# Pooled attention and a tanh-shrink layer on one core: the last two groups' sums on VectorE, the last group's output stored in parts

## The chip, the core and the metric

The kernel runs on one core of a Trainium2 chip. Its time is the device time of one execution in microseconds; lower is better. Where the text gives one number for a kernel, it is the median of its runs, or it is said to be that of the one execution that the profiler recorded. Engines go by their profile names: PE is TensorE (matmuls; PEld its weight loads), DVE is VectorE, ACT is ScalarE, POOL is GpSimd, SP is SyncE, which issues most DMAs.

## The reference

Attention whose keys and values are averaged over 8 neighbours, then a layer with the activation h - tanh(h). Cut to what matters:

```python
# q, k, v: (8, 8, 576, 64) float32;  w_in: (512, 2048);  w_out: (2048, 512)
k_p = k.reshape(B, H, S // 8, 8, D).mean(axis=3)
v_p = v.reshape(B, H, S // 8, 8, D).mean(axis=3)
scores = (1 / sqrt(D)) * q @ k_p.transpose(0, 1, 3, 2)
attn = softmax(scores)
x = (attn @ v_p).transpose(0, 2, 1, 3).reshape(B * S, H * D)   # (4608, 512)
h = x @ w_in
g = h - tanh(h)
out = g @ w_out                                                # (4608, 512)
```

## The kernel before

**Groups.** The 4608 rows of `x` are handled as nine groups of 512 tokens. Groups 0 to 7 hold the first 512 of the 576 tokens of each batch; group 8 holds the last 64 tokens of all eight batches. For each group g, TensorE makes the hidden layer (`h_mms`, line 425), 16 blocks of 128 hidden units; ScalarE takes the tanh of two blocks at a time and VectorE subtracts it (`h_act`, lines 438 and 439), which leaves `gT`: 128 partitions x 16 hidden blocks x 512 tokens in bf16. Then comes the output product with `w2b`. The attention of the next batch is woven in between by a plan written out by hand. Groups 7 and 8 have no next batch (`nb` is None), so their loops hold little but the layer itself.

**Seven products.** Groups 6, 7 and 8 (`SEVEN`) replace the eight quarter products of `g @ w_out` by seven. `gT` is cut into hidden halves (LO, HI) and token halves (C1, C2), `w2b` into hidden halves and column halves (C1, C2). Four sums of quarters of `gT` are needed, made by `g_sum` (line 527): sum 3 (S3), sum 2 (S2, which uses S3), sum 1 (S1), sum 4 (S4, which uses S2). The buffers S1 to S4 lie in `q_raw`. The seven products run on TensorE in the order 4, 2, 7, 1, 6, 5, 3 (`PRODUCTS`), each in two halves of 128 tokens, b = 0 and 1 (`product`, line 545: eight matmuls of 256 columns). Product 7 reads S3, product 6 reads S2, product 5 reads S1, product 3 reads S4. All but product 2 add up in one PSUM bank for each b; nothing is cleared after product 4, so that each bank holds a running sum. After every product the bank is read out (`evacuate`), and the next product on that bank adds to it only after that:

- products 4 and 7: ScalarE copies to `n0` and `n1` (line 560); product 2, which has its own bank, to `p2` (line 558);
- product 1: VectorE subtracts `n1` and writes columns C1 of `o_hs[0]` (line 572); `finish_11` then adds `p2` (line 578);
- product 6: ScalarE copies to columns C1 of `o_hs[1]` (line 562);
- product 5: VectorE subtracts `n0`, columns C2 of `o_hs[1]`; product 3: VectorE subtracts `n1`, columns C2 of `o_hs[0]` (both line 572).

`o_hs[0]` and `o_hs[1]` (shown as `o_h`) each hold one half of the group's output, 128 x 2 x 512 in float32, the middle index being b.

**The order around the change.** Each engine takes its instructions in the order of the program. Within a group of seven products, sum 3 is made while the last hidden blocks are finished. Sum 2 follows when the loop over products is at u = 2, and a manual dependency starts the two halves of sum 1 on GpSimd behind it. Sum 4 follows at u = 8, after both evacuations of product 1. `finish_11` runs on GpSimd, behind sum 1. In groups 6 and 7 each half of the output is stored by one DMA on SyncE's queue (`store_half`, line 588). Group 8's rows are scattered over the batches, and a store needs two DMAs, one for each 64 partitions (line 593): C1 of half 0 after `finish_11`, the whole of half 1 after product 5, both on SyncE, and C2 of half 0 after product 3, one DMA on SyncE and one on ScalarE's queue. That makes six DMAs, five of them on SyncE.

Of the kernel before, what the change touches and what calls it, by code (L numbers as in the profile page):

```python
# [15 lines left out]
B, H, S, D = 8, 8, 576, 64  # L16
POOL = 8
G = S // POOL
DM, DFF = 512, 2048
NHP = H // 2  # L20
R = 4
QA = 128 * R
# [4 lines left out]
NG = 9  # L27
# [4 lines left out]
NQ = NHID // 2  # L32
# [6 lines left out]
def kernel(  # L39
# [9 lines left out]
    nc = tc.nc  # L49
# [49 lines left out]
    o_hs = [const.tile([128, 2, DM], FP32, name=f"o_h{i}") for i in range(2)]  # L99
# [398 lines left out]
    C1, C2 = slice(0, HC), slice(HC, DM)  # L498
# [18 lines left out]
    def g_sum(n, i0, i1, eng=nc.vector):  # L517
        i = slice(i0, i1)
        a11, a12 = gT[:, NQ + i0 : NQ + i1, C1], gT[:, i, C1]
        a21, a22 = gT[:, NQ + i0 : NQ + i1, C2], gT[:, i, C2]  # L520
        o, x, y, op = {
            1: (S1, a21, a22, ALU.add),
            2: (S2, a22, S3[:, i, :], ALU.subtract),
            3: (S3, a11, a21, ALU.subtract),
            4: (S4, a12, S2[:, i, :], ALU.subtract),
        }[n]
        return eng.tensor_tensor(out=o[:, i, :], in0=x, in1=y, op=op)  # L527
# [46 lines left out]
    def finish_11(eng, plain=False):  # L574
        o = o_hs[0][:, :, C1]
        if plain:
            eng.tensor_tensor(out=o, in0=o, in1=n1, op=ALU.subtract)
        eng.tensor_tensor(out=o, in0=o, in1=p2, op=ALU.add)

    def finish_22(eng):  # L580
        o = o_hs[1][:, :, C2]
        eng.tensor_tensor(out=o, in0=o, in1=n0, op=ALU.subtract)

    def store_half(g, hf, cols=slice(0, DM), engs=(nc.sync, nc.sync)):
        o = o_hs[hf]
        if g < B:
            blk = out[g * S : g * S + QA, :].rearrange("(p j) m -> p j m", j=R)
            nc.sync.dma_start(out=blk[:, 2 * hf : 2 * hf + 2, cols], in_=o[:, :, cols])
            return
        tl = out.rearrange("(n t) m -> t n m", t=S)[QA:S, :, :]  # L590
        for e in range(2):
            n = 4 * hf + e
            engs[e].dma_start(
                out=tl[:, n : n + 3 : 2, cols], in_=o[64 * e : 64 * e + 64, :, cols]
            )

    def fill(n, bank, cols=512):
# [26 lines left out]
    for base, sign in ((G, 1), (-1, -1)):  # L624
        nc.gpsimd.affine_select(
            out=mask[:, :, :, 0],
            in_=mask[:, :, :, 0],
# [237 lines left out]
    for g in range(1, NG):  # L865
        nb = g + 1 if g + 1 < B else None
        more = nb is not None and nb + 1 < B

        tail = {2: 0, 3: 1, 5: 2, 7: 3}.get(nb)
        plan = {}  # L870
        if nb is not None:
            units = [(s_block(nb, j), av_block(nb), slot(4 * nb + j)) for j in range(4)]
            s_pairs, a_pairs = [0, 0, 0, 1, 2], [0, 1, 0, 2, 1]
            plan = {
                -12: [("s", 0)],
                -9: [("e", 0)],
                -8: [("s", 1)],
                -5: [("e", 1), ("t", 0)],
                -3: [("s", 2)],
                0: [("e", 2)],  # L880
                1: [("s", 3)],
                3: [("e", 3), ("t", 1)],
                4: [("a", 0)],
                5: [("a", 1), ("x", 0)],
                9: [("a", 2), ("a", 3), ("x", 1)],
            }
            if g == 1:
                plan[-10], plan[-7], plan[-5] = plan.pop(-12), plan.pop(-9), plan.pop(-8)
                plan[-2], plan[-1] = [("e", 1), ("t", 0)], plan.pop(-3)
            if tail is not None:  # L890
                units.append((s_tail(tail), av_tail(tail), slot_tl))
                plan[3].append(("s", 4))
                plan[4] += [("e", 4), ("t", 2)]
                if g == 1:
                    plan[6], plan[7] = plan[4][:1], plan.pop(5)
                    plan[4] = plan[4][1:]
                    plan[10] = plan.pop(9)
                plan[12] = [("a", 4), ("x", 2)]
            if g in SEVEN:
                plan = dict(PLAN7)  # L900
            xs = [x_pair(), x_pair(), x_tl]
        if nb is not None:
            pool_v(nb, nc.gpsimd)
        shs = {}

        def step(kind, n, bk=None):
            if kind == "t2":
                e_turn_dma(units[2][2], n, n + 1)
                return
            if kind == "t":  # L910
                e_turn_dma(units[2 * n][2], 0, 2 if n < 2 else 1)
                if tail and n == 0:
                    turn_tail(tail)
                return
            if kind == "x":
                x_turn_dma(xs[n], *((nb, 2 * n, 2) if n < 2 else (B, tail, 1)))
                return
            s, a, sl = units[n]
            if kind == "s" and bk:
                s_mms(s, bk)  # L920
                ng = s_max(bk)
                late.append(lambda: s_exp_heads(bk, ng, sl))
            elif kind in ("s", "sb"):
                bk = bk or PAIRS[s_pairs[n]]
                s_mms(s, bk)
                shs[n] = s_shift(bk)
            elif kind == "e":
                s_exp(shs[n], sl)
            else:
                bk = bk or PAIRS[a_pairs[n]]  # L930
                av_mms(sl, a, bk)
                normalise(bk, xs[n // 2][:, n % 2, :, :, :])

        for i in range(NHID):
            bk = HB[i // 2 % 3][i % 2] if g in SEVEN else i % 6
            h_mms(g, i, bk)
            if g in SEVEN and i == 15:
                for it in plan.pop(-1, ()):
                    step(*it)
            if i % 2:  # L940
                h_act(i - 1, bk - 1)
                if g in SEVEN:
                    if i in (3, 5) and carry:
                        carry.pop(0)()
                    for n, i0 in {13: [(3, 0)], 15: [(3, 4)]}.get(i, ()):
                        g_sum(n, i0, i0 + 4)
            for it in plan.get(i - NHID, ()):
                step(*it)
            if more and i in (13, 15):
                q_cast(nb + 1, se, i - 13, i - 11)  # L950
        for u in range(14 if g in SEVEN else 0):
            n, b = PRODUCTS[u // 2], u % 2
            product(n, b)
            evacuate(n, b, nb is not None)
            for it in plan.get(u, ()):
                step(*it)
                run_late()
            if u == 2:
                dep = g_sum(2, 0, NQ)
                after([g_sum(1, 0, 4, nc.gpsimd), g_sum(1, 4, NQ, nc.gpsimd)], dep)  # L960
            if u == 8:
                g_sum(4, 0, NQ)
            if b == 0:
                continue
            if n == "1":
                finish_11(nc.gpsimd, nb is not None)
                if g == NG - 1:
                    store_half(g, 0, C1)
            elif g == NG - 1 and n == "5":
                store_half(g, 1)  # L970
            elif g == NG - 1 and n == "3":
                store_half(g, 0, C2, (nc.sync, nc.scalar))
            elif n in "53":
                if n == "5" and nb is not None:
                    finish_22(nc.gpsimd)
                store_half(g, 0 if n == "3" else 1)
        if g in SEVEN and tail is not None:
            carry += [lambda i=tail: tail_values(i), lambda i=tail: x_turn_dma(x_tl, B, i, 1)]
        for u, (tb, qd) in enumerate(() if g in SEVEN else UNITS):
            o_mms(tb, qd * 4, qd * 4 + 4, 4 + tb % 2)  # L980
            if qd == 3:
                o_store(g, tb, 4 + tb % 2, se)
                run(stores)
            for it in plan.get(u, ()):
                step(*it)
            if u == 0 and more:
                pool_k(nb + 1, nc.gpsimd)
            if more:
                if u == 0:
                    q_turn_dma(nb + 1)  # L990
                    run(stores)
                if u == 4:
                    k_turn_dma(nb + 1)
                    k_place_kT(nb + 1, ge)
                if u == 11 and nb % 2 == 0:
                    run(tail_pieces(nb // 2))
                    tail_cast(nb // 2)
            if u == 13:
                load_for(g + 1)
            if g == SEVEN[0] - 1 and u >= 8 and w_ops:  # L1000
                w_ops.pop(0)()
# [29 lines left out]
```

## Time and profile before

| | us |
|---|---|
| median of three runs (lowest, highest) | 306.02 (305.19, 307.4) |
| the profiled execution, its own time | 306.24 |
| span of that execution, first to last instruction | 304.2 |
| TensorE matmul busy | 287.7 (95%) |
| VectorE busy | 202.8 (67%) |
| ScalarE busy | 145.0 (48%) |
| GpSimd busy | 135.4 (45%) |
| end of the last matmul | 297.9 |
| end of the last VectorE instruction | 298.4 |

Starts are counted from the first instruction. A line of the timeline gives start, duration, engine, source line, operation, what is written and what is read, the number of instructions that were merged into it, and in brackets the idle time of the engine before it and what ended that. The chain of waits follows the end of the run back from step to step to whatever released it. A line of a table of stretches gives the stretch, its length, the busy time of PE, PEld, DVE, ACT and POOL (with the number of instructions), the granted TensorE clock, the mean busy share of the 16 DMA engines and the rate in GB/s. For a source line with DMAs, the profile gives the time that the queue spent on issuing each, and the time from there to landing.

### The profile page before, as it was taken

How to read it: one execution, taken by the hardware profiler on the slowest of the kernel's cores; microseconds unless marked ns; L12 is line 12 of the kernel's file. 1: busy time of each engine (PE TensorE's matmuls, PEld its weight loads, DVE VectorE, ACT ScalarE, POOL GpSimd, SP SyncE). 2: the span in 40 equal slices, each digit the busy share in tenths (PEclk: the TensorE clock that was granted, in tenths of full speed). 3: DMA queues.
4: the chain of work that ended last, by engine and by line, in shares of the span. 5: the costliest groups of instructions: out<-in, count | busy, mean ns of one | idle time of the engine just before them, and what ended most of it. 6: DMA issues, size and time to landing. Idle time of an engine off the chain costs nothing.

```text
span 304.2 us, 4875 instructions
## 1 busy us (share of the span) xinstructions
PE 287.7 (95%) x1885; PEld 164.0 (54%) x1885; DVE 202.8 (67%) x283; ACT 145.0 (48%) x199; POOL 135.4 (45%) x112
## 2 busy tenths in 40 slices
PE   5779989899999999999999999999999999999991
PEld 1357865444454455445544454455447854874681
DVE  4586866549853993398329942986699847656861
ACT  2457755347523762366237623672366336416520
POOL 7544918308810692088107910791062920250080
PEclk9599999999999999999999999999999999999998
DMA  7999996789899999896799799959825540021005
GB/s 226 224 218 319 207 290 161 136 254 331 169 218 186 357 180 192 251 314 114 177 254 322 136 155 270 337 63 219 241 65 72 91 160 17 2 99 43 1 0 138
DMA packets 85383, 54.84 MB, mean 180 GB/s; under 512 B 60240, under 2 KB 73168, under 8 KB 85360
## 3 DMA queue, kind: packets, MB, share of 16 engines
q1 hardware_dynamic: 77696, 44.84, 58.7%
q0 software_dynamic: 6400, 8.91, 14.2%
q10 hardware_dynamic: 1264, 0.79, 0.9%
q8 instruction: 14, 0.23, 0.3%
q14 instruction: 9, 0.07, 0.1%
HBM read 36.70 MB, written 9.44 MB: 152 GB/s over the span
## 4 chain that ended last, share of the span: by engine, by line
PE 80%; DVE 10%; DMA 3%; ACT 3%; issue 1%; ACTq 0%; DVEq 0%
PE PS L425 31%; PE PS L468 26%; PE PS L545 11%; PE PS L378 4%; DVE gT L439 3%; PE PS L447 3%; PE PS L291 3%; DMA k_raw<-in_k_dram 2%; DVE sh L306 2%; DVE mx L303 2%; PE PS L272 2%; DMA xT<-x_sb 1%; PE PS L599 1%; DVE x_sb L400 1%; ACT E L342 1%
## 5 line engine op out<-in xcount | busy, mean ns | idle before, releaser
L439 DVE TENSOR_TENSOR gT<-PS,t_sb 128x1024 bf16<-128x1024 f32 x64 | 77.1, 1220 | 42.8 <-ACT t_sb L438 42.8
L425 PE MATMUL PS<-xT,w1b 128*128 128x512 bf16 x448 | 100.8, 379 | 1.0 <-DMA xT<-x_sb 0.9
L468 PE MATMUL PS<-w2b,gT 128*128 128x512 bf16 x384 | 89.8, 379 | 0.2 <-ACT v_sm L782 0.2
L438 ACT ACTIVATE t_sb<-PS 128x1024 f32<-128x1024 f32 x64 | 65.6, 1024 | 49.8 <-PE PS L425 48.4
L425 PEld LDWEIGHTS <-w1b 128*128 128x128 bf16 x512 | 49.1, 98 | 57.6 <-issue 1.9
L468 PEld LDWEIGHTS <-gT 128*128 128x128 bf16 x384 | 35.3, 98 | 37.7 <-issue 0.5
L224 POOL TENSOR_TENSOR v_raw<-v_raw 128x1280 f32<-128x1280 f32 x6 | 17.4, 2906 | 40.8 <-DMA v_raw<-in_v_dram 40.8
L489 ACT COPY o_h<-PS 128x512 f32<-128x512 f32 x22 | 12.8, 584 | 45.9 <-PE PS L468 45.8
L527 POOL TENSOR_TENSOR q_raw<-gT 128x1024 bf16<-128x1024 bf16 x6 | 12.6, 2122 | 44.3 <-PE PS L545 38.5
L303 DVE TENSOR_REDUCE mx<-PS 128x8 f32<-128x576 f32 x36 | 26.9, 748 | 5.8 <-PE PS L291 5.8
L342 ACT ACTIVATE E<-sh 128x576 bf16<-128x576 f32 x32 | 21.8, 680 | 18.5 <-DVE sh L306 18.5
L306 DVE TENSOR_TENSOR sh<-PS,mx 128x576 f32<-128x576 f32 x36 | 27.3, 757 | 1.2
L400 DVE TENSOR_TENSOR x_sb<-PS,rden 128x512 bf16<-128x512 f32 x32 | 22.1, 691 | 1.1
L399 DVE RECIPROCAL rden<-PS 128x8 f32<-128x8 f32 x36 | 7.3, 204 | 22.8 <-PE PS L378 22.7
L209 POOL TENSOR_TENSOR k_raw<-k_raw 128x1280 f32<-128x1280 f32 x7 | 20.3, 2904 | 0.1
L545 PEld LDWEIGHTS <-q_raw 128*128 128x128 bf16 x192 | 18.5, 98 | 2.6 <-DVE q_raw L527 0.4
L246 POOL COPY KB<-kT 64x288 bf16<-64x288 bf16 x12 | 5.1, 422 | 28.6 <-DMA kT<-kd 22.6
L260 ACT CAST q_bf<-q_raw 128x1024 bf16<-128x1024 f32 x14 | 14.4, 1038 | 5.6 <-DMA q_raw<-in_q_dram 5.6
L378 PEld LDWEIGHTS <-ET 128*128 128x128 bf16 x192 | 13.2, 98 | 5.3 <-ACT ET L361 0.8
L378 PE MATMUL PS<-VB,ET 128*128 128x130 bf16 (+2 forms) x192 | 15.8, 221 | 0.2 <-ACT ET L361 0.2
L447 PE MATMUL PS<-xT,w1b 128*128 128x256 bf16 x128 | 15.3, 273 | 0.7 <-ACT xT L417 0.7
L545 PEld LDWEIGHTS <-gT 128*128 128x128 bf16 x144 | 13.9, 98 | 2.0
(95 smaller groups left out, 294.4 us busy)
## 6 DMA issues: line engine op xcount, KB each, us to landing
k_raw<-in_k_dram SPq DMA_DIRECT2D x14, 512.0 KB, 8.5
out_dram<-o_h SPq DMA_DIRECT2D x26, 256.0 KB, 3.1
v_raw<-in_v_dram SPq DMA_DIRECT2D x12, 512.0 KB, 5.0
q_raw<-in_q_dram SPq DMA_DIRECT2D x11, 512.0 KB, 7.0
w1b<-in_moe_w_in_dram POOLq DMA_DIRECT2D x4, 512.0 KB, 8.9
q_raw<-in_q_dram POOLq DMA_DIRECT2D x2, 1024.0 KB, 14.8
w2b<-in_moe_w_out_dram POOLq DMA_DIRECT2D x4, 512.0 KB, 18.9
out_dram<-o_h SPq DMA_DIRECT2D x4, 512.0 KB, 2.8
```

The source lines that it names most:

```text
L209: eng.tensor_tensor(out=r[:, :, 0:4, :], in0=r[:, :, 0:4, :], in1=r[:, :, 4:8, :], op=ALU.add)
L303: nc.vector.reduce_max(out=mx.rearrange("p k h o -> p k (h o)"), in_=sc, axis=AX.X)
L306: nc.vector.tensor_tensor(out=sh[:, :, :, :], in0=sc, in1=mx.to_broadcast([128, 2, 4, G]), op=ALU.subtract)
L342: nc.scalar.activation(out=E[:, e, :, :].rearrange("p t c -> p (t c)")[:, 0:NK], in_=sh.rearrange("p k h c -> p (k h c)"), func=ACT.Exp, s ...
L378: nc.tensor.matmul(PS[ps, banks[half], D1 * h : D1 * (h + s1 - s0)], lhsT=ET[:, t, c0 : c0 + (ps.stop - ps.start)], rhs=VB[kb][:, t, s0:s1 ...
L400: nc.vector.tensor_tensor(out=x_sb, in0=ps[:, :, :, 0:D], in1=rden.to_broadcast([128, 2, 4, D]), op=ALU.mult,)
L425: nc.tensor.matmul(PS[:, bank, :].rearrange("p (j c) -> p j c", j=R), lhsT=w1b[:, fb, i * 128 : (i + 1) * 128], rhs=xT_of(g)[:, :, fb, :], ...
L438: nc.scalar.activation(out=t_sb[:, :, :], in_=ps, func=ACT.Tanh)
L439: nc.vector.tensor_sub(out=gT[:, i : i + 2, :], in0=ps, in1=t_sb[:, :, :])
L447: h_mm_last[0] = nc.tensor.matmul(PS[:, bank, 256 * s : 256 * s + 256].rearrange("p (j c) -> p j c", j=2), lhsT=w1b[:, fb, (2 * n + s) * 1 ...
L468: nc.tensor.matmul(PS[:, bank, 0 : c1 - c0], lhsT=gT[:, i, tb * 128 : (tb + 1) * 128], rhs=w2b[:, i, c0:c1], start=(i == 0), stop=(i == NH ...
L545: nc.tensor.matmul(ps, lhsT=A[:, i, 128 * b : 128 * b + 128], rhs=B_[:, i, :], start=(n in "24" and i == 0), stop=(i == NQ - 1), skip_grou ...
```

## The change

In the last two groups all of sums 2, 1 and 4 are made on VectorE, one after the other, directly behind the subtraction of the last two hidden blocks (i = 15) and sum 3; GpSimd makes no sum there. Group 6 keeps its order. In the last group, `finish_11` runs on VectorE, and the output is stored in parts: C1 of half 0 after product 1, C1 of half 1 after product 6, C2 of half 1 after product 5 (one DMA on SyncE, one on ScalarE), and C2 of half 0 for each b by itself after product 3's evacuation of that b (SyncE and ScalarE each). That makes ten DMAs, seven on SyncE and three on ScalarE. Groups 6 and 7 store as before.

```diff
--- before.py
+++ after.py
@@ -581,17 +581,18 @@
         o = o_hs[1][:, :, C2]
         eng.tensor_tensor(out=o, in0=o, in1=n0, op=ALU.subtract)
 
-    def store_half(g, hf, cols=slice(0, DM), engs=(nc.sync, nc.sync)):
-        o = o_hs[hf]
-        if g < B:
-            blk = out[g * S : g * S + QA, :].rearrange("(p j) m -> p j m", j=R)
-            nc.sync.dma_start(out=blk[:, 2 * hf : 2 * hf + 2, cols], in_=o[:, :, cols])
-            return
+    def store_half(g, hf):
+        blk = out[g * S : g * S + QA, :].rearrange("(p j) m -> p j m", j=R)
+        nc.sync.dma_start(out=blk[:, 2 * hf : 2 * hf + 2, :], in_=o_hs[hf][:, :, :])
+
+    def store_part(hf, cols, b0, b1, engs=(nc.sync, nc.sync)):
+
         tl = out.rearrange("(n t) m -> t n m", t=S)[QA:S, :, :]
         for e in range(2):
-            n = 4 * hf + e
+            n = 4 * hf + 2 * b0 + e
             engs[e].dma_start(
-                out=tl[:, n : n + 3 : 2, cols], in_=o[64 * e : 64 * e + 64, :, cols]
+                out=tl[:, n : n + 2 * (b1 - b0) - 1 : 2, cols],
+                in_=o_hs[hf][64 * e : 64 * e + 64, b0:b1, cols],
             )
 
     def fill(n, bank, cols=512):
@@ -944,6 +945,9 @@
                         carry.pop(0)()
                     for n, i0 in {13: [(3, 0)], 15: [(3, 4)]}.get(i, ()):
                         g_sum(n, i0, i0 + 4)
+                    if i == 15 and nb is None:
+                        for n in (2, 1, 4):
+                            g_sum(n, 0, NQ)
             for it in plan.get(i - NHID, ()):
                 step(*it)
             if more and i in (13, 15):
@@ -955,25 +959,28 @@
             for it in plan.get(u, ()):
                 step(*it)
                 run_late()
-            if u == 2:
+            if nb is not None and u == 2:
                 dep = g_sum(2, 0, NQ)
                 after([g_sum(1, 0, 4, nc.gpsimd), g_sum(1, 4, NQ, nc.gpsimd)], dep)
-            if u == 8:
+            if nb is not None and u == 8:
                 g_sum(4, 0, NQ)
-            if b == 0:
-                continue
-            if n == "1":
-                finish_11(nc.gpsimd, nb is not None)
-                if g == NG - 1:
-                    store_half(g, 0, C1)
-            elif g == NG - 1 and n == "5":
-                store_half(g, 1)
-            elif g == NG - 1 and n == "3":
-                store_half(g, 0, C2, (nc.sync, nc.scalar))
-            elif n in "53":
-                if n == "5" and nb is not None:
-                    finish_22(nc.gpsimd)
-                store_half(g, 0 if n == "3" else 1)
+            if g == NG - 1:
+                if n == "1" and b:
+                    finish_11(nc.vector)
+                    store_part(0, C1, 0, 2)
+                elif n == "6" and b:
+                    store_part(1, C1, 0, 2)
+                elif n == "5" and b:
+                    store_part(1, C2, 0, 2, (nc.sync, nc.scalar))
+                elif n == "3":
+                    store_part(0, C2, b, b + 1, (nc.sync, nc.scalar))
+            elif b:
+                if n == "1":
+                    finish_11(nc.gpsimd, nb is not None)
+                elif n in "53":
+                    if n == "5" and nb is not None:
+                        finish_22(nc.gpsimd)
+                    store_half(g, 0 if n == "3" else 1)
         if g in SEVEN and tail is not None:
             carry += [lambda i=tail: tail_values(i), lambda i=tail: x_turn_dma(x_tl, B, i, 1)]
         for u, (tb, qd) in enumerate(() if g in SEVEN else UNITS):
```

## The prediction

> **What bounds the kernel now.** Read first: the page's busy times, then the chain of waits from group 7 on.
>
> ```profile
> PE 287.7 (95%) x1885; PEld 164.0 (54%) x1885; DVE 202.8 (67%) x283; ACT 145.0 (48%) x199; POOL 135.4 (45%) x112
> ```
> ```profile
> 259.65 12.23 PE PS L545 x112
> 271.88 13.81 PE PS L425 x64
> 285.69 12.24 PE PS L545 x112
> 297.93 0.02 issue
> 297.96 0.42 DVE o_h L572
> ```
>
> TensorE is the bound: from 259.65 to 297.93 the chain holds nothing but matmuls. Any stall of TensorE in the products of group 7 or 8 therefore reaches the end in full. Behind the last matmul lie 0.45 us of VectorE and then 5.8 us (298.38 to 304.2) of stores and closing. Next, the timeline of group 8's products:
>
> ```profile
> 288.78 1.22 DVE L527 TENSOR_TENSOR q_raw<-gT,q_raw 128x2048 bf16<-128x2048 bf16 x1
> 290.17 4.20 POOL L527 TENSOR_TENSOR q_raw<-gT 128x1024 bf16<-128x1024 bf16 x2 [19.66 <-PE PS L545]
> 292.01 0.42 DVE L572 TENSOR_TENSOR o_h<-PS,k_raw 128x256 f32<-128x256 f32 x1 [2.01 <-PE PS L545]
> 292.51 3.66 PE L545 MATMUL PS<-k_raw,q_raw 128*128 128x256 bf16 x32
> 293.13 2.33 DVE L527 TENSOR_TENSOR q_raw<-gT,q_raw 128x2048 bf16<-128x2048 bf16 x1
> 294.32 2.26 POOL L578 TENSOR_TENSOR o_h<-o_h,k_raw 128x512 f32<-128x512 f32 x1
> 296.61 3.56 SPq L593 DMA_DIRECT2D out_dram<-o_h x5
> 297.96 0.42 DVE L572 TENSOR_TENSOR o_h<-PS,k_raw 128x256 f32<-128x256 f32 x1 [0.45 <-PE PS L545]
> 298.41 0.71 ACTq L593 DMA_DIRECT2D out_dram<-o_h x1
> ```
>
> In order: g_sum 2; g_sum 1 on POOL; the evacuation of product 1, b=0, for which VectorE had stood idle 2.01 us; products 6 and 5; g_sum 4; POOL's p2 addition; SP's five issues, which start only when that addition ends (294.32 + 2.26 = 296.58); the last evacuation; ScalarE's one issue. The stores by line, the first and the last one of SP, and DMA activity in quarter microseconds:
>
> ```profile
> L593 SPq DMA_DIRECT2D out_dram<-o_h x1: 685/685/685, 296.6 to 296.6; - x1
> DMA to landing us min/median/max: 2.5/2.5/2.5
> ```
> ```profile
> L593 SPq DMA_DIRECT2D out_dram<-o_h x1: 747/747/747, 299.4 to 299.4; - x1
> DMA to landing us min/median/max: 3.8/3.8/3.8
> ```
> ```profile
> 297.75:298.00 0.25, 0.17 (x2) 0.00 (x0) 0.04 (x1) 0.00 (x0) 0.00 (x0) 1.00 0.13 33
> 298.00:298.25 0.25, 0.00 (x0) 0.00 (x0) 0.25 (x1) 0.00 (x0) 0.00 (x0) 1.00 0.86 209
> 302.50:302.75 0.25, 0.00 (x0) 0.00 (x0) 0.00 (x0) 0.00 (x0) 0.00 (x0) 0.50 0.51 176
> 302.75:303.00 0.25, 0.00 (x0) 0.00 (x0) 0.00 (x0) 0.00 (x0) 0.00 (x0) 0.50 0.05 16
> ```
>
> The last two numbers of a row are DMA share and GB/s. A share of 0.13 in a quarter that then runs at 0.86 puts the first byte at 297.96; 0.05 in the last puts the end near 302.77. Between them all 1 MB of group 8's output moves, back to back. SP's last issue starts at 299.42 (296.61 + 3.56 - 0.75), 1.04 after its data was ready. It lands at 303.22; 0.98 of closing follows. So the tail is set by late stores, held up by POOL.
>
> **The sums (groups 7 and 8).** Both POOL sums go (4.20 a group); VectorE gets one sum of 128x2048, and g_sum 4 moves ahead of the evacuations. In the compiled order, both now stand before the evacuation of product 1, b=0. Price of each: 1.22, from g_sum 2, the same shape. Bounds: 1.22 is the shortest of the six such sums, and 2.33 the longest, which ran while POOL had its sums. I take 1.22, since POOL has no work then. VectorE starts back-to-back instructions 0.02 to 0.04 apart. Group 8: g_sum 2 ends at 290.00; + 2 x 1.22 + 0.09 = 292.53, against 292.01: the evacuation is 0.52 late. Behind it waits TensorE, since product 6, b=0, adds into that bank. Before, the evacuation ended at 292.43, and a hand-over from VectorE to TensorE takes 0.05 (group 6: g_sum 3 ends at 234.85, its weight load begins at 234.90), so 292.51 had 0.03 to spare: a stall of 0.49. Group 7 by the same rows: 262.74 + 1.23 = 263.97; + 2 x 1.23 + 0.09 = 266.52 against 265.97, less 0.03: 0.52. The b=1 evacuation adds nothing: 0.42 of VectorE against eight matmuls (0.87) on b=0. Together **+1.01 us on TensorE**; at 2.33 a sum it would be 2.71 + 2.74 = 5.45, at the other end (no stall) 0. POOL's relief is worth nothing on the path: S1 was ready in time (products 6 and 5 ran without a gap).
>
> **The p2 addition on VectorE (group 8).** Price 0.69:
>
> ```profile
> L209 DVE TENSOR_TENSOR k_raw<-k_raw x3: 426/686/692, 4.7 to 9.7; 128x512 f32<-128x512 f32 x2, 128x256 f32<-128x256 f32 x1
> ```
>
> With group 7's 0.52, product 1's evacuations run from 293.05 to 293.91, the addition to 294.64. VectorE's next work is product 5's b=0 at 295.38 + 1.01 = 296.39: that gap of 1.75 covers it; without cover it would cost 0.69. The first stores can be issued at 294.67 instead of 296.61.
>
> **The stores.** Six become ten, seven on SP and three on ScalarE, all in pieces of 1 KB. SP, at 0.60 to 0.75 an issue: C1 of half 0 from 294.67 to 295.95; C1 of half 1 (last evacuation at 294.46 + 0.37 + 1.01 = 295.84) to 297.3; C2 of half 1 (ready 296.63 + 1.01 = 297.64) from 297.67 to 298.3; C2 of half 0, b=0 (ready 298.51) from 298.54 to 299.2; b=1 (ready 298.38 + 1.01 = 299.39) from 299.42. ScalarE issues beside SP, at 0.71. By chance the last issue starts when it started before; what changes is how soon it lands. By the compiled order it also waits for the landing of C1's second store (295.3 + 2.5 = 297.8), past by then.
>
> Data starts 1.35 after issue (296.61 to 297.96), and 1 KB pieces move at some 195 GB/s (298 to 299.25, the C1 stores of before). C1: 296.02 to 297.36; half 1, C1: to 298.8; half 1, C2: 299.02 to 300.36; the last 256 KB: to 301.7, against 302.77. Landing 0.45 later (302.77 to 303.22): 302.15, which is 2.7 after issue instead of 3.8. From TensorE's end to the span's end it was 304.2 - 297.93 = 6.27; it becomes 0.45 of evacuation, 0.03 to the issue, 2.7 to the landing and 0.98 of closing, 4.16: **-2.1 us on the tail**. Bounds of the last landing: 2.5 (empty rings, first row) and 3.9 (ScalarE's store of before), so -2.3 to -0.9; I take 2.7, nearest to the first row, as the rings hold little when it is issued.
>
> Group 7's stores are issued 0.5 later with their evacuations; only group 8's evacuations into the same halves, 17 us on, wait for their landing (2.6 after issue): nothing.
>
> Here the Trainium skill (DMA: Bandwidth & Descriptors, Measured) speaks against the change: it advises batching to 1 MiB, and gives 0.95 us for 64 KB (there, of a load), the size of the last four stores. No run here shows a 64 KB store; four of 0.95 in turn would, as an estimate, end the data at 303.7 and the kernel near 307.2, while my rows give 305.1. Its mechanism is the fourth rival, priced there by rows.
>
> **Sum.** +1.01 - 2.1 = -1.1. The profiled execution took 306.24 (span 304.2, 2.04 around it); 306.24 - 1.1 = **305.1 us**, span 303.1. The median shown, 306.02, lies 0.2 below that execution; runs scatter from 305.19 to 307.4, so I leave it.
>
> **The rivals.**
> 1. No stall: VectorE would have to do each sum 0.26 faster than any row shows. Then -2.1: 304.1. Chance 0.10.
> 2. The last landing is no shorter, rings not drained: 3.8 again, 306.2. For it: ScalarE's store took 3.9 with 0.5 MB ahead; against it: half of the output is now away by 299. Chance 0.12.
> 3. Slower, from sums at 2.33 each: stalls of 5.45 less 2.1, so 309.5. It decides from stalls of 2.1 together, 1.5 a sum. For it: group 6's sum took 1.43 beside POOL; against it: POOL idle. Chance 0.06.
> 4. Slower, from small stores: the last four, of 64 KB, do not overlap, and each takes from first byte to landing as long as SP's first store (2.5 - 1.35 = 1.15). They begin at 299.9, so the last lands at 304.5: 304.5 + 0.98 + 2.04 = 307.5. It decides from 0.83 each, where the last lands at 303.22 as before. For it: GB/s falls with the piece (some 400 in group 7's 4 KB pieces, 195 at 1 KB); against it: the pieces of these stores stay at 1 KB, and the six stores of before moved back to back with no gap between them. Chance 0.10.
>
> The forecast keeps 0.62, its own range 304.3 to 305.9. The range reaches to rivals 1 and 2, with some scatter, and leaves out 3 and 4 (0.16): 303.8 to 306.9. About 1%, 3 us, is what a measurement of this kernel can tell from no change: faster by that needs rival 1 and a good run (0.03); slower is rival 3 and little else (0.07); within 0.90.
>
> **What would show it.** In the changed profile: two more 1.22 us rows at line 527 behind g_sum 2; the first line-572 row after them 0.5 late in both groups, and a gap of TensorE of 0.5 before product 6, released by VectorE; SP's first store at 294.7; the last landing about 2.7 after issue. No gap of TensorE, sums near 2.3, or a last landing over 3.5 would make the prediction wrong.

## The result and the profile after

The changed kernel takes 304.18 us (median of nine runs, 303.56 to 305.47); the kernel before took 305.57 us in nine runs (305.19 to 307.4). The ratio is 0.9949, 95% interval 0.9926 to 0.9971: 1.6 us faster by the ratio, between 0.9 and 2.3 (the medians alone differ by 1.4). That is a change of half a per cent, clear of the scatter of nine runs a side. The forecast was 305.1 with a range of 303.8 to 306.9, and no change to be told at 1%.

The profiled execution took 304.10 us, span 302.4 instead of 304.2. The page's busy times and the chain of waits, as shown of before:

```profile
PE 287.3 (95%) x1885; PEld 163.5 (54%) x1885; DVE 203.5 (67%) x286; ACT 144.9 (48%) x199; POOL 123.8 (41%) x107
```
```profile
259.34 12.37 PE PS L545 x112
271.71 13.81 PE PS L425 x64
285.52 12.38 PE PS L545 x112
297.91 0.02 issue
297.93 0.42 DVE o_h L572
```

POOL is busy 11.6 us less. The products of groups 7 and 8 take 12.37 and 12.38 instead of 12.23 and 12.24: TensorE does stall, by 0.14 in each group. After the last matmul 4.5 us are left instead of 6.3. The timeline of group 8's products (start, duration, what runs, idle time before and what ended it):

```profile
288.61 1.22 DVE L527 TENSOR_TENSOR q_raw<-gT,q_raw 128x2048 bf16<-128x2048 bf16 x1
289.75 1.22 DVE L527 TENSOR_TENSOR q_raw<-gT 128x2048 bf16<-128x2048 bf16 x1
290.89 1.22 DVE L527 TENSOR_TENSOR q_raw<-gT,q_raw 128x2048 bf16<-128x2048 bf16 x1
292.02 0.42 DVE L572 TENSOR_TENSOR o_h<-PS,k_raw 128x256 f32<-128x256 f32 x1
292.49 3.65 PE L545 MATMUL PS<-k_raw,q_raw 128*128 128x256 bf16 x32
293.07 0.69 DVE L578 TENSOR_TENSOR o_h<-o_h,k_raw 128x512 f32<-128x512 f32 x1
293.80 5.88 SPq L593 DMA_DIRECT2D out_dram<-o_h  x7
295.31 0.42 DVE L572 TENSOR_TENSOR o_h<-PS,k_raw 128x256 f32<-128x256 f32 x1 [1.54 <-PE PS L545]
296.64 2.76 ACTq L593 DMA_DIRECT2D out_dram<-o_h  x3
297.93 0.42 DVE L572 TENSOR_TENSOR o_h<-PS,k_raw 128x256 f32<-128x256 f32 x1 [0.45 <-PE PS L545]
```

Sums 2, 1 and 4 each last 1.22, but start 1.14 apart. The p2 addition ends at 293.76, and SP's first store goes out at once. SP's last store, and the DMA activity around it:

```profile
L593 SPq DMA_DIRECT2D out_dram<-o_h x1: 818/818/818, 298.9 to 298.9; - x1
DMA to landing us min/median/max: 2.3/2.3/2.3
```
```profile
298.75:299.00 0.25, 0.00 (x0) 0.00 (x0) 0.00 (x0) 0.00 (x0) 0.00 (x0) 1.00 0.98 332
299.00:299.25 0.25, 0.00 (x0) 0.00 (x0) 0.00 (x0) 0.00 (x0) 0.00 (x0) 1.00 0.14 41
299.25:299.50 0.25, 0.00 (x0) 0.00 (x0) 0.00 (x0) 0.00 (x0) 0.00 (x0) 1.00 0.21 66
300.50:300.75 0.25, 0.00 (x0) 0.00 (x0) 0.00 (x0) 0.00 (x0) 0.00 (x0) 1.00 0.64 160
```

Data now ends near 300.8 instead of 302.8. But the last evacuation ended at 298.35 and its store started only at 298.9, and from 299.0 to 299.5, before its data moved, the DMA engines ran nearly dry (0.14 and 0.21 busy). The pair before, for b=0, had taken SP 1.26 us and ScalarE 1.24 us to issue, where 0.6 to 0.75 had been expected.

Where the 1.8 us of span went, both kernels measured alike: group 7's first product starts 0.31 earlier (259.18 against 259.49), in a part that the change does not touch, so scatter; the two stalls cost 0.28; from the last matmul to the span's end it is 4.5 instead of 6.3, 1.8 less. The thirteen profiled executions of this document reach group 7 anywhere between 258.8 and 259.9, so the experiments are read by three lengths of their profiles: the two groups' products, the stretch from group 7's first product to the span's end (44.71 before, 43.22 after), and the tail from the last product's end. Spans are given to 0.1 us, so stretches and tails are good to 0.05.

### The profile page after: what moved, and what is told of

Its sections match the earlier page's. It is cut to its first block, busy times and chain, and to the rows that moved or that the text cites. A ratio compares the mean times of both kernels' runs of the same rounds, so it can differ in the third digit from the quotient of the medians.

```text
span 302.4 us, 4875 instructions
## 1 busy us (share of the span) xinstructions
PE 287.3 (95%) x1885; PEld 163.5 (54%) x1885; DVE 203.5 (67%) x286; ACT 144.9 (48%) x199; POOL 123.8 (41%) x107
## 3 DMA queue, kind: packets, MB, share of 16 engines
q1 hardware_dynamic: 77856, 44.71, 59.4%
## 4 chain that ended last, share of the span: by engine, by line
PE 79%; DVE 10%; DMA 5%; ACT 3%; issue 1%; ACTq 0%; DVEq 0%
PE PS L425 32%; PE PS L468 25%; PE PS L545 11%; PE PS L378 4%; PE PS L447 3%; DVE gT L439 3%; PE PS L291 3%; DMA k_raw<-in_k_dram 2%; DMA xT<-x_sb 2%; DVE sh L306 2%; DVE mx L303 2%; PE PS L272 1%; ACT E L342 1%; DVE x_sb L400 1%; ACT t_sb L438 1%
## 5 line engine op out<-in xcount | busy, mean ns | idle before, releaser
L291 PEld LDWEIGHTS <-qT 128*128 128x128 bf16 x128 | 9.9, 98 | 8.8 <-issue 1.6
```

## The experiments

Two theories were to be told apart. First: SP was held up by POOL, so that either edit that frees POOL or goes round it brings most of the gain. Second: the gain comes from storing in smaller parts. Later two more questions came up: why the stall was so small, and why one pair of stores was slow to issue. The edits are cut to the lines that change. All lengths stand in one table, in us; "load" says where a 16 KB packet of the instruction queue moved near the end, which is taken up below:

| kernel | stall, groups 7 / 8 | tail | stretch | median (ratio, interval) | load |
|---|---|---|---|---|---|
| before | 0 / 0 | 6.3 | 44.71 | 1 | after the span |
| changed | 0.14 / 0.14 | 4.5 | 43.22 | 304.18 (0.9949, 0.9926 to 0.9971) | in the stores |
| changed again | 0.14 / 0.14 | 4.25 | 42.96 | 304.05 (0.9936, 0.9924 to 0.9949) | in the stores |
| sums only | 0.14 / 0.14 | 5.0 | 43.71 | 305.19 (0.9973, 0.9958 to 0.9987) | not seen |
| stores only | 0 / 0.43 | 4.25 | 43.11 | 304.39 (0.9952, 0.9934 to 0.9969) | after the span |
| last block whole | 0.14 / 0.14 | 4.4 | 43.12 | 303.80 (0.9925, 0.9903 to 0.9948) | not seen |
| sum 4 late | 0 / 0 | 4.0 | 42.44 | 303.36 (0.9914, 0.9889 to 0.9940) | not seen |
| sum 4 late, again | 0 / 0 | 4.0 | 42.47 | 303.85 (0.9936, 0.9913 to 0.9960) | after the span |
| sum 4 late, last block whole | 0 / 0 | 4.4 | 42.82 | 303.91 (0.9923, 0.9902 to 0.9944) | after the span |
| sums in the order 2, 4, 1 | 0.27 / 0.26 | 4.0 | 42.97 | 304.60 (one run) | after the span |
| padded on GpSimd | 0.14 / 0.14 | 4.05 | 42.76 | 304.61 (one run) | after the span |
| padded on ScalarE | 0.14 / 0.14 | 4.0 | 42.69 | 304.26 (one run) | after the span |
| padded on TensorE | 0.14 / 0.14 | 4.8 | 43.51 | 304.76 (one run) | in the stores |

**The sums alone.** On the kernel before:

```diff
+                    if i == 15 and nb is None:
+                        for n in (2, 1, 4):
+                            g_sum(n, 0, NQ)
-            if u == 2:
+            if nb is not None and u == 2:
-            if u == 8:
+            if nb is not None and u == 8:
```

> The sums of groups 7 and 8 on VectorE as in the changed kernel, the stores and the p2 addition as before (POOL). Measure: the stretch from group 7's first product (line 545) to the span's end, 44.71 us before, 43.22 in the changed kernel. Theory 1 (what helps is that POOL, with no sums, releases SP earlier; parts of the output are of little account): stall of 0.14 a group, POOL's addition 1.27 from 293.1 on, SP's first store near 294.4, last pair at 298.4 with the rings half empty, stretch 43.4 to 43.6, ratio to before 0.9960. Theory 2 (the parts are what helps): the last store lands 3.8 after its issue as before, stretch 44.2 or more, ratio 0.999 to 1.001.

Timeline of this kernel:

```profile
293.63 1.27 POOL L578 TENSOR_TENSOR o_h<-o_h,k_raw 128x512 f32<-128x512 f32 x1 [24.86 <-DVE o_h L572]
294.92 4.57 SPq L593 DMA_DIRECT2D out_dram<-o_h  x5
```

POOL, without sums of its own to finish first, waits only for VectorE's evacuation, adds in 1.27 instead of 2.26, and SP starts 3.48 before the last matmul's end (298.40) where it was 1.31 before. The tail falls by 1.3 and the stretch by 1.0: 43.71 lies just above the first theory's 43.4 to 43.6 and well under the second's 44.2. The ratio, 0.9973, is weaker than its 0.9960, which the interval still holds.

**The stores and the addition alone.** On the changed kernel, the sums put back:

```diff
-                    if i == 15 and nb is None:
-                        for n in (2, 1, 4):
-                            g_sum(n, 0, NQ)
-            if nb is not None and u == 2:
+            if u == 2:
-            if nb is not None and u == 8:
+            if u == 8:
```

> The stores in parts and the p2 addition on VectorE as in the changed kernel, the sums as before (two on POOL, sum 4 after product 1). Theory 1: no stall of TensorE, the addition ends by about 294, SP is free as early as in the changed kernel: stretch 42.9, 0.3 below the changed kernel, ratio 0.9935. Theory 2 (VectorE and POOL in each other's way): the addition, with two operands in SBUF, waits for POOL's sums (to 294.4) and pushes sum 4 (before 295.46) towards product 3 (296.0): addition near 1.5 us, a gap of TensorE before product 3 of up to 0.8, stretch 43.3 to 43.8.

Timeline of this kernel, VectorE behind product 1 and TensorE at product 3:

```profile
292.95 1.67 DVE L578 TENSOR_TENSOR o_h<-o_h,k_raw 128x512 f32<-128x512 f32 x1
294.54 1.21 DVE L527 TENSOR_TENSOR q_raw<-gT,q_raw 128x2048 bf16<-128x2048 bf16 x1
295.68 0.74 DVE L572 TENSOR_TENSOR o_h<-PS,k_raw 128x256 f32<-128x256 f32 x2
296.14 1.91 PE L545 MATMUL PS<-w2b,q_raw 128*128 128x256 bf16 x16 [0.26 <-DVE o_h L572]
```

The addition takes 1.67 beside POOL's sums against 0.69 in the changed kernel, sum 4 and product 5's evacuation come late, and product 3 starts 0.43 late. So the second expectation names the mechanism, while the stretch, 43.11, falls between the two (42.9; 43.3 to 43.8). Still the tail falls by 2.0. The edits alone take 1.0 and 1.6 of stretch; both together take 1.5 (1.75 in the second profile, 2.0 in two padded kernels below). They do not add up, since both remove the same wait, SP's for POOL. But the parts count too: "sums only" has a tail of 5.0, the padded kernels, which have the same sums, 4.0. How much of that 1.0 belongs to the parts and how much to the addition on VectorE, no run here separates.

**The last block stored whole.** On the changed kernel:

```diff
-                elif n == "3":
-                    store_part(0, C2, b, b + 1, (nc.sync, nc.scalar))
+                elif n == "3" and b:
+                    store_part(0, C2, 0, 2, (nc.sync, nc.scalar))
```

> The changed kernel, but the last block (C2 of half 0) is stored as before, one pair of 128 KB after both evacuations of product 3. In the changed kernel the pair for b=0 took 1.25 us to issue on both queues, so that the last pair started at 298.9, 0.5 after its data. Theory 1 (the split by b gives nothing back): last pair at 298.4, landing 2.5 to 2.8 later, stretch 43.0 to 43.3. Theory 2 (the split helps): landing 3.3 or more after issue, stretch 43.7 or more.

Last pair at 297.98, landing 2.6 and 2.8 later, stretch 43.12: as the first theory has it, and beside this profile of the changed kernel the split gains nothing. The same edit without the stall, below, shows why that is not the whole answer.

**Sum 4 behind product 1's evacuation again.** On the changed kernel:

```diff
-                        for n in (2, 1, 4):
+                        for n in (2, 1):
-            if nb is not None and u == 8:
+            if u == 8:
```

> The changed kernel, but sum 4 stands behind the evacuations of product 1 again (on VectorE, alone). Theory: the gap of 0.14 before product 6 in each group comes from sum 4 ahead of the evacuation, so it goes: products of groups 7 and 8 12.24 each instead of 12.37, stretch 42.94, 0.28 below the changed kernel, tail unchanged at 4.5. Rival: product 1's evacuation is still late or sum 4 comes too late for product 3: stretch 43.2 or more.

The stall is gone in both groups, as expected: VectorE waits 0.87 for product 1 instead of being late. The tail was expected unchanged at 4.5 and came out at 4.0; here the pair for b=0 took 0.49 and 0.74 to issue. The changed kernel itself was therefore profiled once more.

**The changed kernel again, and the two variants beside it on one chip.**

> The changed kernel itself, for a second profile. In its first one the pair of stores for b=0 took 1.25 us to issue on both queues, and DMA activity sank to 0.14 of the engines at 299.0 before the last pair moved. Theory 1 (that belongs to the pattern: both queues issue small stores at the same instant): 1.2 us again, tail from TensorE's end 4.5. Theory 2 (a hiccup of that one execution, as the same pair took 0.49 and 0.74 with sum 4 late): 0.75 or less, last pair within 0.1 of its data, tail 4.0 to 4.2. Stall 0.14 a group either way.

The pair took 1.06 and 1.04, the last pair started 0.3 after its data, the tail was 4.25. So it recurs; the hiccup of one execution is out. The exact 1.2 and 4.5 do not recur.

> Sum 4 behind product 1's evacuation, and the last block stored whole, in one pair of 128 KB. Beside the kernel with sum 4 late alone, it prices the split by b without stall. Theory 1 (the split is worth what the smaller last pair lands earlier): last landing 2.7 after issue against 2.1, tail 4.3 to 4.4 against 4.0, median 0.3 to 0.5 above that kernel. Theory 2 (the split is worth nothing): tail 4.0 to 4.1, medians within 0.2.

(The edits of the two kernels above together.) Tail 4.4 against 4.0: the split by b is worth some 0.4 of stretch when the issue is not slow. The medians, 303.91 against 303.85, expected 0.3 to 0.5 apart, do not show it; its runs scatter from 303.0 to 305.4.

> The kernel with sum 4 late once more, beside the changed kernel on the same chip. Theory: no gap before product 6 (products 12.23 and 10.48), tail 4.0, median 0.3 us below the changed kernel if the slow issue was a hiccup, 0.8 below if it belongs to the changed kernel.

Products without a gap, tail 4.0, stretch 42.47 against 42.44 in its first profile. The median is 0.2 below that of the changed kernel beside it (303.85 and 304.05), below either figure expected, and the intervals overlap. By its profiles this version is 0.5 to 0.8 faster than the changed kernel; by medians the two are not told apart on that chip.

**The order of the sums.** On the changed kernel:

```diff
-                        for n in (2, 1, 4):
+                        for n in (2, 4, 1):
```

> The changed kernel with the sums in the order 2, 4, 1 in groups 7 and 8, so that sum 4, which reads sum 2's result, stands right behind it. Theory 1 (a VectorE instruction that needs nothing of the one before starts 0.09 before that one's end, one that does starts 0.04 after it): sum 2 to sum 4 1.26 instead of 1.14, evacuation 0.12 later, TensorE's gap 0.26 to 0.28 a group instead of 0.14. Theory 2 (instructions follow each other at 1.14 whatever they read): gap 0.14 as in the changed kernel.

Timeline of this kernel; the two sums of the first line are 2 and 4:

```profile
289.49 2.49 DVE L527 TENSOR_TENSOR q_raw<-gT,q_raw 128x2048 bf16<-128x2048 bf16 x2
291.89 1.22 DVE L527 TENSOR_TENSOR q_raw<-gT 128x2048 bf16<-128x2048 bf16 x1
293.02 0.90 DVE L572 TENSOR_TENSOR o_h<-PS,k_raw 128x256 f32<-128x256 f32 x2
```

Sum 4, which reads sum 2's result, no longer overlaps it (2.49 for the two); sum 1, which needs neither, starts 0.09 before their end (289.49 + 2.49 = 291.98). The stall grows to 0.27 and 0.26: the first theory, in its number.

**What makes the pair slow.** The DMA table of a stretch lists queues with packets, MB and share of the engines' time. In the changed kernel, from 297.00 to 297.25, and in its second profile, from 297.25 to 297.50, it has a line that the others lack there:

```profile
q8 instruction: 1, 0.02, 27.8%
```
```profile
q8 instruction: 1, 0.02, 21.9%
```

One packet of 16 KB of instructions, some 0.9 to 1.1 us on one DMA engine (27.8% of 16 engines for 0.25 us is 1.1; the table counts a packet whole in the stretch in which it starts). In the other kernels so far it moved after the span or not at all. Three kernels lengthen one engine's program behind all else, each by four idle instructions, to see whether the packet moves:

```diff
+    for _ in range(4):
+        nc.gpsimd.memset(zeros[0:1, 0:2], 0.0)
```

> The changed kernel with four tiny fills on GpSimd behind everything else, which only make its program longer. In both profiles of the changed kernel one 16 KB packet of the instruction queue moves at 297.4 or 297.7, amid the last stores; in the other kernels it moves after the span or is not seen. Theory 1 (that instruction load, whose place hangs on the program's length and layout, holds one DMA engine and makes the pair for b=0 slow): if the load leaves the stores, that pair issues in 0.75 or less and the tail from TensorE's end is 4.0; if it stays, 1.0 or more and 4.2 to 4.5. Theory 2 (the pattern of the stores is slow by itself): 1.0 or more wherever the load lies.

> The same with four tiny copies on ScalarE behind its last store. Theory 1: the slow issue goes with the instruction load: load amid the stores, 1.0 or more and a tail of 4.2 to 4.5; load elsewhere, 0.75 or less and 4.0. Theory 2: 1.0 or more in any case.

(With `nc.scalar.copy(out=warm[0:1, :], in_=warm[0:1, :])` in the loop.)

> The same with four small matmuls on TensorE behind the last product (some 0.1 us, beside the stores; the tail is counted from the last product's end). Theory 1: the slow issue goes with the instruction load: load amid the stores, 1.0 or more and a tail of 4.2 to 4.5; load elsewhere, 0.75 or less and 4.0. Theory 2: 1.0 or more in any case.

(With `fill(4, 7, 64)` instead.) Padded on GpSimd or ScalarE, the packet moves after the span; the pair for b=0 issues in 0.49 and 0.66 or 0.67, the tail is 4.05 and 4.0. Padded on TensorE, the packet stays, at 298.0; the pair issues in 0.49 and 0.65 all the same, but stores land late, and the tail is 4.8. SP's fourth store of the kernel padded on GpSimd, then of the one padded on TensorE, then of the changed kernel in its first profile:

```profile
L593 SPq DMA_DIRECT2D out_dram<-o_h x1: 605/605/605, 296.1 to 296.1; - x1
DMA to landing us min/median/max: 2.4/2.4/2.4
```
```profile
L593 SPq DMA_DIRECT2D out_dram<-o_h x1: 604/604/604, 296.2 to 296.2; - x1
DMA to landing us min/median/max: 4.0/4.0/4.0
```
```profile
L593 SPq DMA_DIRECT2D out_dram<-o_h x1: 603/603/603, 295.9 to 295.9; - x1
DMA to landing us min/median/max: 3.7/3.7/3.7
```

So the tail goes with the packet: 4.25, 4.5 and 4.8 with it amid split stores, 4.0 to 4.05 in five kernels with the split stores and without it, two of which are the changed kernel but for the padding. ("Stores only" has 4.25 without it: its first store goes out 0.8 later, after the slow addition, and SP's issues run into each other.) The pattern of the stores is not slow by itself. The slow issue, by which the expectations wanted to tell, shows in only two of the three profiles with the packet. The sign that all three share is the late landing: SP's fourth store lands 3.7, 3.5 and 4.0 after its issue there, and 2.4 in those five. What sets the packet's place, and how it reaches the issue on the queues, stays open.

The time of the whole execution does not show this gain: the two kernels whose packet left the stores took 304.61 and 304.26 in their single runs (on another chip), the two profiled executions of the changed kernel 304.10 and 304.05. Where the packet ends more than 2 us after the span, the time outside the span follows it. It is 2.05 before, 1.77 in "stores only", 2.55 and 2.75 padded on GpSimd and ScalarE, and 2.86 with sum 4 late and the last block whole, in each of the five 0.3 less than the distance from the span's end to the packet's (2.35, 2.08, 2.85, 3.06, 3.18); in the other eight profiles it is 1.7 to 1.85. No run varies this alone. But by these rows the padding took the packet from one place where it costs time to another.

## Why the prediction was right or wrong

**The bound and the place of the tail: right.** TensorE's chain is whole but for the two gaps, and the tail shrank because SP was released by VectorE near 293.8 instead of by POOL at 296.6. "Sums only", which leaves the stores as they were, shows the earlier release to be worth 1.3 of the tail; with the parts and the addition on VectorE it is 1.8, and 2.3 where no packet moves amid the stores.

**The sums, +1.01: right in mechanism, wrong in size.** The late evacuation and the stall before product 6 are there, but measure 0.28. The price of 1.22 a sum was right. The step that failed is "+ 2 x 1.22 + 0.09", which set the instructions end to end with gaps of 0.02 to 0.04. From sum 2's start to the evacuation it made 3.75; the trace shows 3.41, three spacings of 1.14. Against 3.23 before, that is 0.18 late instead of 0.52, and less the 0.03 to spare 0.15, close to the 0.14 measured. The gaps had been read from instructions that use the result of the one ahead; the order 2, 4, 1 shows that only these wait for its end. The profile before already had the other case, product 1's second evacuation in group 8:

```profile
292.79 0.42 DVE L572 TENSOR_TENSOR o_h<-PS,k_raw 128x256 f32<-128x256 f32 x1 [0.35 <-PE PS L545]
```

It ends at 293.21, and sum 4, which needs nothing of it, starts at 293.13.

**The p2 addition on VectorE, hidden at 0.69: right.** It measured 0.69 and delayed nothing: VectorE still waited 1.54 for product 5. The cover of 1.75 had been read from an evacuation that sum 4 held back before. Its condition, POOL idle, carries the price: beside POOL's sums it took 1.67 and cost a gap of 0.43. The Trainium skill (GPSIMD Engine Reference, Key points) says that GpSimd shares its SBUF interfaces with VectorE and is in contention with VectorE instructions that have two SBUF inputs. The 1.67 against 0.69 agrees, as do POOL's 2.26 and 1.27.

**The stores, -2.1: right in direction, 1.8 measured.** Ten stores went out in the order and nearly at the distances worked out. The last one landed 2.3 after issue, not 2.7, but was issued 0.5 after its data, which the working did not have, and which went with the instruction load. Without it the tail is 4.0, against 4.16 worked out. The closing after the last landing was set at 0.98; it measures 1.2 to 1.3 behind pairs of 64 KB and 1.0 to 1.1 behind 128 KB. The profile doesn't show what fills it.

**The sum.** +0.28 - 1.8 = -1.5, where +1.01 - 2.1 = -1.1 had been forecast; two misses of opposite sign, 0.73 and 0.3, partly cancel, which is luck. The measured gain, 0.9 to 2.3, holds both. The 305.1 was added up from one execution of 306.24; the profiled execution of the changed kernel took 304.10, 1.0 less than forecast. Of that, 0.4 is the sum, 0.3 lies ahead of group 7, and 0.3 outside the span (1.7 instead of 2.04): two parts that the prediction took as they were.

**The rivals.** The first, no stall, has with 304.1 the time nearest to the 304.18, but not its condition: the sums are not 0.26 shorter each, they overlap by 0.08, and the stall is 0.28. The second, no shorter landing, is out (2.3). The third, sums at 2.33 (its 309.5 adds up to 309.6), is out: all are 1.22. The fourth, small stores served in turn, is out: 64 KB stores land 2.0 to 2.7 after issue without the load. The advice of the Trainium skill that was weighed there (DMA: Bandwidth & Descriptors, Measured), to batch, is not borne out at the end of this kernel: without the packet, storing the last block in two steps ends some 0.4 sooner, since only the last step's bytes come after the last result.

## What to carry to other kernels

Ask of a tail first who released the queue, and only then how many bytes it moves: here the same 1 MB was released 2.8 sooner, and its data ended 2.0 sooner. Two edits that remove the same wait don't add up, so price them together. And when work is moved ahead of an evacuation that TensorE waits for, count start-to-start distances of independent instructions, and put the sum that is needed last behind the evacuation.

## What the runs showed of the hardware

- VectorE starts an instruction that needs nothing of the one before about 0.08 ahead of that one's recorded end (1.14 apart at 1.22 each); one that does starts 0.03 to 0.04 after it.
- An instruction load of 16 KB amid the output stores went with 0.25 to 0.8 us more of tail. Four idle instructions at the end of GpSimd's or ScalarE's program moved it behind the span, where it went with 0.8 to 1.0 us more time outside the span (one run each).
- A pair of 64 KB stores lands 2.0 to 2.7 us after issue, a pair of 128 KB 2.4 to 3.0, when little lies ahead of it and no instruction load moves beside it.
